# Transposes beside the output accumulators: a dynamic convolution and a two-matmul block on one Trainium2 core

## The chip, the cores and the metric

The kernel runs on one core of a Trainium2 chip (trn2). Times are device microseconds of one execution. The engines are named as in the profile: PE is TensorE's matmul, PEld its weight load, DVE is VectorE, ACT is ScalarE, POOL is GpSimd, SP issues most of the DMAs.

## The reference, cut to what matters

```python
# x (8, 4096, 192), weight_gen (8, 4096, 8 heads, 7), w_in (192, 2048), w_out (2048, 192)
w = softmax(weight_gen)                       # over the 7 taps, for each token and head
x_pad = concat(zeros(6 tokens), x)            # causal window of 7 tokens
conv[b, s, h, g] = sum_k w[b, s, h, k] * x_pad[b, s + k, h, g]     # 24 channels in a head
h = conv.reshape(32768, 192) @ w_in
out = (h - tanh(h)) @ w_out
```

## The kernel before

**Tiling.** The 32,768 tokens are cut into 32 superblocks of 1,024 tokens; a partition holds 8 consecutive tokens (J = 8). The work of a superblock is a convolution, whose result is transposed so that channels lie on partitions (`convT`), a first matmul (`gemm1`, 16 tiles f of 128 hidden columns), tanh and subtraction, and a second matmul (`gemm2`, 8 blocks of 128 tokens).

**Convolution.** ScalarE takes the exponential of the weights (`softmax_exp`, L117). VectorE sums over the taps and takes the reciprocal (`softmax_norm`, L127 and L131). GpSimd multiplies the exponentials by the reciprocal (`wsm`, L138), and then makes seven products of x and the weights of one tap, 128x1536 each (L156), into three tiles: `even` (taps 0, 2, 4), `odd` (1, 3, 5) and `last` (6). A DMA from GpSimd's queue then adds most of `odd` onto `even` (L165). TensorE transposes and sums what is left in PSUM by matmuls with the identity (`conv`, L194): 104 matmuls of 64x64 a superblock, in two groups, for channel chunks (0, 1) and (2,). The matmuls work in pairs: row tile r = 0 takes partitions 0 to 63, r = 1 takes 64 to 127, each with a PSUM bank of its own. ScalarE copies each group to `convT` (L204). For superblock 0 five of the seven products are VectorE's (taps 1, 3, 4, 5, 6).

**Matmuls.** `gemm1(n, f)` fills a tile `ph` of two banks (L217); ScalarE takes its tanh (`th`, L226) and VectorE subtracts (`gt`, L228). `gemm2(i)` multiplies block i by the upper half of w_out's contraction rows (r = 0), in a new bank `po`, and finishes block i-1 (r = 1) in the bank of the call before (L248); ScalarE then copies the finished block to `out_sb` (L273). A `po` tile is a whole bank of 512 columns, of which 192 are used.

**PSUM.** [...] `psum_h` has three slots of two banks, for `ph` and for the transposes' `pc` alike; `psum_o` has two slots of one bank for `po`. The tiles of most SBUF pools have two buffers.

**Order.** The order of each engine's instructions is written out by hand. In superblock n the loop over p = 0 to 7 issues two gemm1 tiles and, for the superblock before, one gemm2. GpSimd makes the products of superblock n+2, SP loads superblock n+3. The exponential of n+3 stands at p = 1, its sum and reciprocal at p = 2. The transposes of superblock n+1 stand at p = 2 and 5, up to n = 3 both at p = 7:

```python
if n + 1 < NTOT:
    if p == (2 if n > 3 else 7):
        conv(n + 1, (0, 1))
    if p == (5 if n > 3 else 7):
        conv(n + 1, (2,))
```

An engine works through its instructions in order: where one waits, all behind it wait.

Of the kernel before, what the change touches and what calls it, by code (L numbers as in the profile page):

```python
# [8 lines left out]
FP32 = mybir.dt.float32  # L9
BF16 = mybir.dt.bfloat16  # L10

ACT = mybir.ActivationFunctionType
# [4 lines left out]
def kernel(  # L17
# [8 lines left out]
    nc = tc.nc  # L26
# [15 lines left out]
    NFT = F // P  # L42
    NC = D // R
    GC = G // NC
    NPAIR = K // 2
    ACC = NPAIR * J * D - J * R
    assert S % TOK == 0 and D % R == 0 and H * GC == R and F % P == 0
# [19 lines left out]
    wg_of = {}  # L67
    e_of = {}
    zr_of = {}
    prods_of = {}  # L70
    conv_of = {}
    g_of = {}
# [48 lines left out]
        )  # L121
        e_of[n] = e_t

    def softmax_norm(n):
        e_t = e_of.pop(n)
        zsum = wgpool.tile([P, J * H], FP32, name="zsum")
        nc.vector.reduce_sum(  # L127
            out=zsum[:], in_=e_t[:].rearrange("p j h k -> p (j h) k"), axis=AX.X
        )
        zr = wgpool.tile([P, J * H], FP32, name="zr")  # L130
        nc.vector.reciprocal(zr[:], zsum[:])  # L131
        zr_of[n] = (e_t, zr)

    def products(n, on_vector=(), hooks={}):
        x_t = x_of.pop(n)
        e_t, zr = zr_of.pop(n)
        wsm = wgpool.tile([P, J, H, K], FP32, name="wsm")
        nc.gpsimd.tensor_mul(  # L138
            wsm[:].rearrange("p j h k -> p (j h) k"),
            e_t[:].rearrange("p j h k -> p (j h) k"),  # L140
            zr[:].rearrange("p (n o) -> p n o", o=1).to_broadcast([P, J * H, K]),
        )

        even = ppool.tile([P, NPAIR, NC, J, H, GC], BF16, name="even")
        odd = ppool.tile([P, NPAIR, NC, J, H, GC], BF16, name="odd")
        last = ppool.tile([P, NC, J, H, GC], BF16, name="last")
        dst = {}
        for i in range(NPAIR):
            dst[2 * i] = even[:, i]
            dst[2 * i + 1] = odd[:, i]  # L150
        dst[K - 1] = last[:]
        if -1 in hooks:
            hooks[-1]()
        for k in range(K):
            eng = nc.vector if k in on_vector else nc.gpsimd
            eng.tensor_mul(  # L156
                dst[k].rearrange("p c j h g -> p j h c g"),
                x_t[:, k : k + J, :].rearrange("p j (h c g) -> p j h c g", h=H, c=NC),
                wsm[:, :, :, k : k + 1]
                .rearrange("p j h (k o) -> p j h k o", o=1)  # L160
                .to_broadcast([P, J, H, NC, GC]),
            )
            if k == K - 2:

                nc.gpsimd.dma_start(  # L165
                    out=even[:].rearrange("p i c j h g -> p (i c j h g)")[:, 0:ACC],
                    in_=odd[:].rearrange("p i c j h g -> p (i c j h g)")[:, 0:ACC],
                    accum_op=mybir.AluOpType.add,
                    max_dma_last_dim=4096,
                )  # L170
            if k in hooks:
                hooks[k]()
        groups = [even[:, i] for i in range(NPAIR)] + [last[:]]
        prods_of[n] = [groups + ([odd[:, NPAIR - 1]] if c == NC - 1 else []) for c in range(NC)]

    def conv(n, chunks):

        prods = prods_of[n]
        if n not in conv_of:
            conv_of[n] = cpool.tile([P, NC, HT], BF16, name="convT")  # L180
        convT = conv_of[n]
        nch = len(chunks)
        pc = psum_h.tile([P, 2, HT], FP32, name="pc", tag="ph")
        steps = [
            (gi, ci, c)
            for gi in range(NPAIR + 2)
            for ci, c in enumerate(chunks)
            if gi < len(prods[c])
        ]
        for si, (gi, ci, c) in enumerate(steps):  # L190
            for j in range(JH):
                col = (ci * JH + j) * R
                for r in range(2):
                    nc.tensor.matmul(  # L194
                        pc[:, r, col : col + R],
                        lhsT=prods[c][gi][r * R : (r + 1) * R, c, 2 * j : 2 * j + 2].rearrange(
                            "p j h g -> p (j h g)"
                        ),
                        rhs=ident[r * R : (r + 1) * R, r * R : (r + 1) * R],
                        start=(si == 0 and j == 0),  # L200
                        stop=(si == len(steps) - 1 and j == JH - 1),
                    )
        c0 = chunks[0]
        nc.scalar.activation(  # L204
            out=convT[:, c0 : c0 + nch, :].rearrange("p c (j r t) -> p r (c j) t", r=2, t=R),
            in_=pc[:, :, 0 : nch * JH * R].rearrange("p r (cj t) -> p r cj t", t=R),
            func=ACT.Copy,
        )
        if c0 + nch == NC:
            prods_of.pop(n)  # L210

    def gemm1(n, f):
        convT = conv_of[n]
        ph = psum_h.tile([P, 2, HT], FP32, name="ph", tag="ph")
        for c in range(NC):
            for r in range(2):
                nc.tensor.matmul(  # L217
                    ph[:, r, :],
                    lhsT=w_in[r * R : (r + 1) * R, c, f * P : (f + 1) * P],
                    rhs=convT[r * R : (r + 1) * R, c, :],  # L220
                    start=(c == 0),
                    stop=(c == NC - 1),
                )
        th = tpool.tile([P, TOK], FP32, name="th")
        ph_f = ph[:].rearrange("p r t -> p (r t)")
        last_act[0] = nc.scalar.activation(out=th[:], in_=ph_f, func=ACT.Tanh)  # L226
        gt = gpool.tile([P, TOK], BF16, name=f"gt{f}", tag=f"gt{f}")
        nc.vector.tensor_sub(gt[:], ph_f, th[:])  # L228
        g_of.setdefault(n, []).append(gt)
# [5 lines left out]
    def gemm2(i):  # L235

        ops = []
        for r, blk in ((0, i), (1, i - 1)):
            if not 0 <= blk < LAST:
                continue  # L240
            n, j = divmod(blk, J)
            if r == 0:
                half[blk] = psum_o.tile([P, 512], FP32, name="po")
            ops.append((r, n, j, half[blk]))
        for f in range(NFT):
            for r, n, j, po in ops:
                col = (j % 2) * HT + (j // 2) * P
                mm = nc.tensor.matmul(  # L248
                    po[:, 0:D],
                    lhsT=g_of[n][f][r * R : (r + 1) * R, col : col + P],  # L250
                    rhs=w_out[r * R : (r + 1) * R, f, :],
                    start=(r == 0 and f == 0),
                    stop=(r == 1 and f == NFT - 1),
                )
                if r == 1 and f == 0 and i in (1, LAST):


                    tc.add_manual_dep(
                        mm.ins,
                        last_act[0].ins.name,  # L260
                        mybir.DependencyInfo(
                            mybir.DependencyClass.Sync, mybir.DependencyReason.DATA
                        ),
                        reason="order of the row tiles in a bank",
                    )
        if i > 0:
            blk = i - 1
            n, j = divmod(blk, J)
            po = half.pop(blk)
            if j == 0:  # L270
                out_of[n] = opool.tile([P, J, D], FP32, name="out_sb")
            out_sb = out_of[n]
            last_act[0] = nc.scalar.activation(out=out_sb[:, j, :], in_=po[:, 0:D], func=ACT.Copy)  # L273
            if j == J - 1:
                out_of.pop(n)
                g_of.pop(n)
                nc.sync.dma_start(
                    out=out[n * TOK : (n + 1) * TOK, :].rearrange("(p j) e -> p j e", p=P),
                    in_=out_sb[:],
                )  # L280
# [62 lines left out]
    for n in range(NTOT):  # L343
        if n + 3 < NTOT:
            load(n + 3)
        if n + 2 < NTOT:
            products(n + 2)
        for p in range(J):
            gemm1(n, 2 * p)
            gemm1(n, 2 * p + 1)  # L350
            if p == 1 and n + 3 < NTOT:
                softmax_exp(n + 3)
            if n >= 1:
                gemm2((n - 1) * J + p)
            if n + 1 < NTOT:
                if p == (2 if n > 3 else 7):
                    conv(n + 1, (0, 1))
                if p == (5 if n > 3 else 7):
                    conv(n + 1, (2,))
            if p == 2 and n + 3 < NTOT:  # L360
                softmax_norm(n + 3)
    gemm2(LAST)
    for j in range(J):
        gemm2_last(j)
# [30 lines left out]
```

The softmax here doesn't subtract the row's maximum and nothing guards it: scores larger than these inputs give would overflow.

## Time and profile before

| | |
|---|---|
| median of 3 runs | 806.3 us (803.76 to 807.86) |
| profiled execution | 803.36 us, of which the span is 801.5 us |
| TensorE clock granted | 0.997 of full speed |
| busy in the span: PE, DVE, ACT, POOL | 738.3, 653.4, 644.2, 707.2 us |
| transposes (L194), matmuls | 3,328 |
| copies to convT (L204) | 32 of 1,024 ns, 32 of 597 ns |
| wsm on POOL (L138) | 32 of 1,392 ns |
| adding DMA even<-odd | 32, 8.9 us from issue to landing |

A busy share is an average over the whole span. The timeline of a stretch gives the start and the duration of each instruction, merged where several of a kind follow each other ("x12"), and in brackets how long the engine was idle before it and what ended the idle time. The chain that ended last is followed back from the last instruction: at each step to what released it.

### The profile page before, as it was taken

The numbers are of one execution on the slowest core, as the hardware profiler recorded it, in microseconds if no ns is written. First come the engines' busy times: TensorE is split into PE (matmuls) and PEld (weight loads), VectorE is DVE, ScalarE is ACT, GpSimd is POOL, SyncE is SP. The second block draws the span as 40 slices with busy tenths as digits, with TensorE's granted clock in tenths as the row PEclk, the third lists the DMA queues.
The fourth block names the chain that finished last, engine by engine and source line by source line (L and its number), as shares of the span: only waits on it lengthen the run. The fifth ranks groups of instructions, "written<-read, shape, count | busy, mean of one in ns | idle before, by whom it ended". The sixth has DMA issues, their size and how long they took to land.

```text
span 801.5 us, 31993 instructions
## 1 busy us (share of the span) xinstructions
PE 738.3 (92%) x14592; PEld 570.1 (71%) x14592; DVE 653.4 (82%) x590; ACT 644.2 (80%) x865; POOL 707.2 (88%) x298
## 2 busy tenths in 40 slices
PE   0269999799999999999999999999999999999997
PEld 0227777577777777777777777777777777777777
DVE  5397877688888888888888888888888888887883
ACT  0187888688888888888888888888888888888883
POOL 7799999999999999999999999999999999996000
PEclk9999999999999999999999999999999999999999
DMA  8785555566665555576656654675654556634112
GB/s 165 220 172 119 106 136 152 150 171 174 175 170 112 141 147 149 155 175 174 170 128 147 141 149 146 168 174 143 156 147 125 150 155 175 163 55 95 42 41 81
DMA packets 25990, 114.50 MB, mean 143 GB/s; under 512 B 4688, under 2 KB 9344, under 8 KB 21704
## 3 DMA queue, kind: packets, MB, share of 16 engines
q1 hardware_dynamic: 14576, 77.34, 28.1%
q0 software_dynamic: 11280, 35.13, 27.1%
q8 instruction: 114, 1.87, 1.0%
q14 instruction: 20, 0.16, 0.1%
HBM read 54.49 MB, written 25.17 MB: 99 GB/s over the span
## 4 chain that ended last, share of the span: by engine, by line
PE 74%; DVE 13%; ACT 5%; DMA 4%; POOL 3%; issue 1%; SPq 0%; DVEq 0%; POOLq 0%; ACTq 0%
PE ph L217 35%; PE po L248 34%; DVE gt L228 11%; ACT th L226 4%; PE pc L194 4%; DMA even<-odd 3%; PE po L289 1%; POOL even L156 1%; POOL odd L156 1%; DMA x_t<-in_x_dram 1%; DVE odd L156 1%; POOL last L156 0%; ACT convT L204 0%; DVE even L156 0%; DVE zr L131 0%
## 5 line engine op out<-in xcount | busy, mean ns | idle before, releaser
L228 DVE TENSOR_TENSOR gt<-ph,th 128x1024 bf16<-128x1024 f32 x512 | 602.2, 1219 | 110.7 <-ACT th L226 107.8
L226 ACT ACTIVATE th<-ph 128x1024 f32<-128x1024 f32 x512 | 500.6, 1023 | 62.1 <-PE ph L217 57.1
L217 PE MATMUL ph<-convT,w_in 64*128 64x512 bf16 x3072 | 391.0, 377 | 17.8 <-DVE gt L228 16.1
L248 PEld LDWEIGHTS <-gt 64*128 64x128 bf16 x7936 | 344.3, 94 | 54.1 <-ACT th L226 1.7
L248 PE MATMUL po<-w_out,gt 64*128 64x192 bf16 x7936 | 374.6, 243 | 2.5 <-ACT th L226 1.3
L156 POOL TENSOR_TENSOR even<-x_t,wsm 128x1536 bf16<-128x1536 f32 x95 | 277.9, 2925 | 7.6 <-POOL wsm L138 6.1
L156 POOL TENSOR_TENSOR odd<-x_t,wsm 128x1536 bf16<-128x1536 f32 x93 | 269.9, 2902 | 0.0
L217 PEld LDWEIGHTS <-w_in 64*128 64x128 bf16 x3072 | 169.6, 94 | 133.3 <-issue 43.4
L156 POOL TENSOR_TENSOR last<-x_t,wsm 128x1536 bf16<-128x1536 f32 x31 | 104.3, 3364 | 0.0
L273 ACT ACTIVATE out_sb<-po 128x192 f32<-128x192 f32 x248 | 82.1, 331 | 19.1 <-PE po L248 13.1
L204 ACT ACTIVATE convT<-pc 128x1024 bf16<-128x1024 f32 x64 | 51.4, 810 | 45.8 <-PE pc L194 45.7
L194 PE MATMUL pc<-ident,even 64*128 64x64 bf16 x2304 | 46.6, 192 | 39.2 <-DMA even<-odd 38.9
L194 PEld LDWEIGHTS <-even 64*128 64x128 bf16 x2304 | 43.6, 97 | 39.9 <-issue 39.6
L165 POOL DMA_DIRECT2D even<-odd x32 | 38.6, 1205 | 13.5 <-POOL odd L156 9.6
L138 POOL TENSOR_TENSOR wsm<-e_t,zr 128x448 f32<-128x448 f32 x32 | 44.5, 1392 | 5.1 <-DVE zr L131 5.1
L117 ACT ACTIVATE e_t<-wg_t 128x448 f32<-128x448 f32 x32 | 18.5, 578 | 18.4 <-DMA wg_t<-in_weight_gen_dram 18.4
L127 DVE TENSOR_REDUCE zsum<-e_t 128x64 f32<-128x448 f32 x32 | 19.5, 609 | 16.6 <-ACT e_t L117 16.6
L194 PE MATMUL pc<-ident,last 64*128 64x64 bf16 x768 | 23.6, 193 | 0.0
L131 DVE RECIPROCAL zr<-zsum 128x64 f32<-128x64 f32 x32 | 17.7, 553 | 3.1
L194 PEld LDWEIGHTS <-last 64*128 64x128 bf16 x768 | 17.3, 97 | 0.1
L156 DVE TENSOR_TENSOR odd<-x_t,wsm 128x1536 bf16<-128x1536 f32 x3 | 7.9, 2654 | 5.0 <-DMA x_t<-in_x_dram 5.0
L289 PE MATMUL po<-w_out,gt 64*128 64x192 bf16 x256 | 11.0, 243 | 0.0
(17 smaller groups left out, 47.2 us busy)
## 6 DMA issues: line engine op xcount, KB each, us to landing
even<-odd POOLq DMA_DIRECT2D x32, 1024.0 KB, 8.9
x_t<-in_x_dram SPq DMA_DIRECT2D x24, 1344.0 KB
out_dram<-out_sb SPq DMA_DIRECT2D x31, 768.0 KB
x_t<-in_x_dram SPq DMA_DIRECT2D x8, 1176.0 KB
wg_t<-in_weight_gen_dram SPq DMA_DIRECT2D x32, 224.0 KB
x_t<-in_x_dram SPq DMA_DIRECT2D x8, 157.5 KB
w_in<-in_moe_w_in_dram POOLq DMA_DIRECT2D x8, 96.0 KB, 5.7
w_in<-w_in SPq DMA_DIRECT2D x2, 384.0 KB
```

The source lines that it names most:

```text
L127: nc.vector.reduce_sum(out=zsum[:], in_=e_t[:].rearrange("p j h k -> p (j h) k"), axis=AX.X)
L138: nc.gpsimd.tensor_mul(wsm[:].rearrange("p j h k -> p (j h) k"), e_t[:].rearrange("p j h k -> p (j h) k"), zr[:].rearrange("p (n o) -> p n ...
L156: eng.tensor_mul(dst[k].rearrange("p c j h g -> p j h c g"), x_t[:, k : k + J, :].rearrange("p j (h c g) -> p j h c g", h=H, c=NC), wsm[:, ...
L165: nc.gpsimd.dma_start(out=even[:].rearrange("p i c j h g -> p (i c j h g)")[:, 0:ACC], in_=odd[:].rearrange("p i c j h g -> p (i c j h g)" ...
L194: nc.tensor.matmul(pc[:, r, col : col + R], lhsT=prods[c][gi][r * R : (r + 1) * R, c, 2 * j : 2 * j + 2].rearrange("p j h g -> p (j h g)") ...
L204: nc.scalar.activation(out=convT[:, c0 : c0 + nch, :].rearrange("p c (j r t) -> p r (c j) t", r=2, t=R), in_=pc[:, :, 0 : nch * JH * R].re ...
L217: nc.tensor.matmul(ph[:, r, :], lhsT=w_in[r * R : (r + 1) * R, c, f * P : (f + 1) * P], rhs=convT[r * R : (r + 1) * R, c, :], start=(c == ...
L226: last_act[0] = nc.scalar.activation(out=th[:], in_=ph_f, func=ACT.Tanh)
L228: nc.vector.tensor_sub(gt[:], ph_f, th[:])
L248: mm = nc.tensor.matmul(po[:, 0:D], lhsT=g_of[n][f][r * R : (r + 1) * R, col : col + P], rhs=w_out[r * R : (r + 1) * R, f, :], start=(r == ...
L273: last_act[0] = nc.scalar.activation(out=out_sb[:, j, :], in_=po[:, 0:D], func=ACT.Copy)
L289: nc.tensor.matmul(po[:, r, 0:D], lhsT=g_of[n][f][r * R : (r + 1) * R, col : col + P], rhs=w_out[r * R : (r + 1) * R, f, :], start=(f == 0 ...
```

## The change

- The transposes of superblock n+1 (n >= 1) no longer take a slot of `psum_h`. They are cut into three groups, one for a channel chunk, at p = 2, 4 and 6 from n = 1 on (`conv_beside`), and write columns 192 to 447 of the two `po` banks that gemm2 has just used: r = 0 in that of block i, r = 1 in that of block i-1. Each group has two copies to `convT`, one for a bank. Superblocks 0 and 1 still use `conv`.
- The exponential of superblock n+3 moves to p = 4, its sum and reciprocal to p = 6. From superblock 4 on the reciprocal is written to columns 448 to 511 of block i's `po` bank, and VectorE, not GpSimd, multiplies it with the exponentials.
- For superblock 0 VectorE makes its own scaled weights, in a slot of `psum_h`, and GpSimd makes those of its two products.
- For superblocks 0, 1 and 2 (`PLAIN`) the adding DMA is left out. TensorE sums all seven products, 168 matmuls in place of 104, in the order in which the products come.

```diff
+    PLAIN = (0, 1, 2)
...
-    def softmax_norm(n):
+    def softmax_norm(n, po=None):
...
+        zr = po[:, 512 - J * H : 512]
+        nc.vector.reciprocal(zr, zsum[:])
+        wsm = wgpool.tile([P, J, H, K], FP32, name="wsm")
+        scale(nc.vector, wsm[:], e_t, zr)
+        wsm_of[n] = wsm
...
+            if on_vector:
+                pw = psum_h.tile([P, 2, HT], FP32, name="pw", tag="ph")
+                wsm_v = pw[:, 0, 0 : J * H * K].rearrange("p (j h k) -> p j h k", j=J, h=H)
+                scale(nc.vector, wsm_v, e_t, zr[:])
+            wsm = wgpool.tile([P, J, H, K], FP32, name="wsm")
+            scale(nc.gpsimd, wsm[:], e_t, zr[:])
+        in_pairs = n not in PLAIN
...
-            eng = nc.vector if k in on_vector else nc.gpsimd
+            eng, w = (nc.vector, wsm_v) if k in on_vector else (nc.gpsimd, wsm[:])
...
-            if k == K - 2:
+            if k == K - 2 and in_pairs:
                 nc.gpsimd.dma_start(
...
+            prods_of[n] = [[dst[k] for k in sorted(range(K), key=lambda k: (k in on_vector, k))]] * NC
...
+    def conv_beside(n, c, pos):
+        convT = conv_tile(n)
+        banks = [po[:, D : D + JH * R] for po in pos]
+        transposes(n, (c,), banks, False)
+        for r in range(2):
+            nc.scalar.activation(
+                out=convT[:, c, :].rearrange("p (j r t) -> p r j t", r=2, t=R)[:, r],
+                in_=banks[r].rearrange("p (j t) -> p j t", t=R),
+                func=ACT.Copy,
+            )
...
-            if p == 1 and n + 3 < NTOT:
+            if p == 4 and n + 3 < NTOT:
                 softmax_exp(n + 3)
             if n >= 1:
-                gemm2((n - 1) * J + p)
-            if n + 1 < NTOT:
-                if p == (2 if n > 3 else 7):
-                    conv(n + 1, (0, 1))
-                if p == (5 if n > 3 else 7):
-                    conv(n + 1, (2,))
-            if p == 2 and n + 3 < NTOT:
-                softmax_norm(n + 3)
+                gemm2(i)
+            if n == 0 and p == J - 1:
+                conv(1, (0, 1))
+                conv(1, (2,))
+            elif n >= 1 and n + 1 < NTOT and p in (2, 4, 6):
+                conv_beside(n + 1, p // 2 - 1, (half[i], half[i - 1]))
+            if p == 6 and n + 3 < NTOT:
+                softmax_norm(n + 3, half[i] if n >= 1 else None)
```

`scale` is the multiplication that `products` held before, on the engine that it is given. `transposes` holds the matmul loop of `conv` before, and writes to the banks that it is given; beside gemm2's columns its first matmul does not carry the start flag[...].

More of the change, by code (lines that the diff above doesn't have):

```diff
@@ L69 @@
     zr_of = {}
+    wsm_of = {}
     prods_of = {}
@@ L129, in softmax_norm, with scale @@
         )
-        zr = wgpool.tile([P, J * H], FP32, name="zr")
-        nc.vector.reciprocal(zr[:], zsum[:])
-        zr_of[n] = (e_t, zr)
+        if po is None:
+            zr = wgpool.tile([P, J * H], FP32, name="zr")
+            nc.vector.reciprocal(zr[:], zsum[:])
+            zr_of[n] = (e_t, zr)
+            return
+        zr = po[:, 512 - J * H : 512]
[3 more added lines that the diff above has]
+        wsm_of[n] = wsm
+    def scale(eng, wsm, e_t, zr):
+        eng.tensor_mul(
+            wsm.rearrange("p j h k -> p (j h) k"),
+            e_t[:].rearrange("p j h k -> p (j h) k"),
+            zr.rearrange("p (n o) -> p n o", o=1).to_broadcast([P, J * H, K]),
+        )
     def products(n, on_vector=(), hooks={}):
         x_t = x_of.pop(n)
[L136 to L142, printed above, removed]
+        wsm_v = None
+        if n in wsm_of:
+            wsm = wsm_of.pop(n)
+        else:
+            e_t, zr = zr_of.pop(n)
+            if on_vector:
[5 more added lines that the diff above has]
+        in_pairs = n not in PLAIN
         even = ppool.tile([P, NPAIR, NC, J, H, GC], BF16, name="even")
@@ L158, in products @@
                 x_t[:, k : k + J, :].rearrange("p j (h c g) -> p j h c g", h=H, c=NC),
-                wsm[:, :, :, k : k + 1]
+                w[:, :, :, k : k + 1]
                 .rearrange("p j h (k o) -> p j h k o", o=1)
@@ L172, in products @@
                 hooks[k]()
[L173 to L178, printed above, removed]
+        if in_pairs:
+            groups = [even[:, i] for i in range(NPAIR)] + [last[:]]
+            prods_of[n] = [
+                groups + ([odd[:, NPAIR - 1]] if c == NC - 1 else []) for c in range(NC)
+            ]
+        else:
+            prods_of[n] = [[dst[k] for k in sorted(range(K), key=lambda k: (k in on_vector, k))]] * NC
@@ L179, in conv, with conv_tile, transposes @@
+    def conv_tile(n):
         if n not in conv_of:
             conv_of[n] = cpool.tile([P, NC, HT], BF16, name="convT")
-        convT = conv_of[n]
+        return conv_of[n]
+    def transposes(n, chunks, banks, start):
+        prods = prods_of[n]
+        steps = [
+            (gi, ci, c, j)
+            for gi in range(max(len(prods[c]) for c in chunks))
+            for ci, c in enumerate(chunks)
+            if gi < len(prods[c])
+            for j in range(JH)
+        ]
+        for si, (gi, ci, c, j) in enumerate(steps):
+            col = (ci * JH + j) * R
+            for r in range(2):
+                nc.tensor.matmul(
+                    banks[r][:, col : col + R],
+                    lhsT=prods[c][gi][r * R : (r + 1) * R, c, 2 * j : 2 * j + 2].rearrange(
+                        "p j h g -> p (j h g)"
+                    ),
+                    rhs=ident[r * R : (r + 1) * R, r * R : (r + 1) * R],
+                    start=(start and si == 0),
+                    stop=(si == len(steps) - 1),
+                    skip_group_check=not start,
+                )
+        if chunks[-1] == NC - 1:
+            prods_of.pop(n)
@@ L182, in conv @@
+    def conv(n, chunks):
+        convT = conv_tile(n)
         nch = len(chunks)
         pc = psum_h.tile([P, 2, HT], FP32, name="pc", tag="ph")
[L184 to L202, printed above, removed]
+        transposes(n, chunks, (pc[:, 0], pc[:, 1]), True)
@@ L208, in conv @@
         )
-        if c0 + nch == NC:
-            prods_of.pop(n)
+    def conv_beside(n, c, pos):
+        convT = conv_tile(n)
+        banks = [po[:, D : D + JH * R] for po in pos]
+        transposes(n, (c,), banks, False)
+        for r in range(2):
+            nc.scalar.activation(
+                out=convT[:, c, :].rearrange("p (j r t) -> p r j t", r=2, t=R)[:, r],
+                in_=banks[r].rearrange("p (j t) -> p j t", t=R),
+                func=ACT.Copy,
+            )
     def gemm1(n, f):
@@ L265, in gemm2 @@
                     )
+        half.pop(i - 2, None)
         if i > 0:
@@ L268, in gemm2 @@
             n, j = divmod(blk, J)
-            po = half.pop(blk)
+            po = half[blk]
             if j == 0:
@@ L348 @@
         for p in range(J):
+            i = (n - 1) * J + p
             gemm1(n, 2 * p)
             gemm1(n, 2 * p + 1)
-            if p == 1 and n + 3 < NTOT:
+            if p == 4 and n + 3 < NTOT:
                 softmax_exp(n + 3)
             if n >= 1:
-                gemm2((n - 1) * J + p)
-            if n + 1 < NTOT:
-                if p == (2 if n > 3 else 7):
-                    conv(n + 1, (0, 1))
-                if p == (5 if n > 3 else 7):
-                    conv(n + 1, (2,))
-            if p == 2 and n + 3 < NTOT:
-                softmax_norm(n + 3)
+                gemm2(i)
[6 more added lines that the diff above has]
+                softmax_norm(n + 3, half[i] if n >= 1 else None)
     gemm2(LAST)
```

## Prediction

> **What bounds the kernel now.** I read the page first (shares, then the chain that ended last), then TensorE's timeline of one steady superblock with ScalarE's and VectorE's beside it, then GpSimd's start.
>
> From the page:
>
> ```profile
> PE 738.3 (92%) x14592; PEld 570.1 (71%) x14592; DVE 653.4 (82%) x590; ACT 644.2 (80%) x865; POOL 707.2 (88%) x298
> ...
> PE 74%; DVE 13%; ACT 5%; DMA 4%; POOL 3%; issue 1%; SPq 0%; DVEq 0%; POOLq 0%; ACTq 0%
> ...
> L204 ACT ACTIVATE convT<-pc 128x1024 bf16<-128x1024 f32 x32 | 32.8, 1024 | 38.9 <-PE pc L194 38.9
> ```
>
> TensorE carries 74% of the chain. Now its timeline around the second transpose group of a superblock (start, duration, engine, line):
>
> ```profile
> 338.71 1.48 PE L217 MATMUL ph<-convT,w_in 64*128 64x512 bf16 x12
> 340.00 1.50 PE L248 MATMUL po<-w_out,gt 64*128 64x192 bf16 x32
> 341.32 0.53 PE L194 MATMUL pc<-ident,even 64*128 64x64 bf16 x24
> 341.67 0.30 PE L194 MATMUL pc<-ident,last 64*128 64x64 bf16 x8
> 341.79 0.30 PE L194 MATMUL pc<-ident,odd 64*128 64x64 bf16 x8
> 341.91 0.83 PE L217 MATMUL ph<-convT,w_in 64*128 64x512 bf16 x6
> 343.04 0.82 PE L217 MATMUL ph<-convT,w_in 64*128 64x512 bf16 x6 [0.30 <-DVE gt L228]
> ```
>
> Starts tell more than durations, since ends are modelled. A pair of gemm1 tiles issues in 1.29 us, a gemm2 in 1.32, so one p takes 2.61; the 40 transposes take 0.59 (14.6 ns each), the 64 of the other group 0.93. TensorE runs without a hole up to 341.91. Eight p and 104 transposes make 8 x 2.61 + 1.52 = **22.4 us**; the measured period is 23.12 (VectorE's pair after the second group starts at 340.63, 363.75, 386.86). The missing 0.7 us is the price of lending an h slot to each of the two transpose groups: 0.30 in the last line, the rest in slower gemm1 pairs after each group. What runs beside:
>
> ```profile
> 339.57 1.94 ACT L226 ACTIVATE th<-ph 128x1024 f32<-128x1024 f32 x2 [0.32 <-PE ph L217]
> 341.54 0.33 ACT L273 ACTIVATE out_sb<-po 128x192 f32<-128x192 f32 x1
> ...
> 352.92 0.58 ACT L117 ACTIVATE e_t<-wg_t 128x448 f32<-128x448 f32 x1
> 353.39 0.33 ACT L273 ACTIVATE out_sb<-po 128x192 f32<-128x192 f32 x1
> ```
>
> ```profile
> 340.63 2.36 DVE L228 TENSOR_TENSOR gt<-ph,th 128x1024 bf16<-128x1024 f32 x2 [0.33 <-ACT th L226]
> ```
>
> With the p's first gemm1 at 338.71 as zero, gemm2 is issued by +2.61, the copy of its finished block to out_sb ends at +3.16, the gt pair ends at +4.28. The transposes at 341.32 did not wait for that copy: they had a tile of their own.
>
> In the chain before 150 us the limit is GpSimd and its adding DMA:
>
> ```profile
> 132.48 2.87 POOL odd L156
> 135.35 0.29 issue
> 135.65 9.34 DMA even<-odd
> 144.99 0.14 issue
> 145.12 1.89 PE pc L194 x64
> 147.01 1.93 PE ph L217 x12
> ```
>
> GpSimd's period is 22.64 us (wsm at 48.73, 71.38, 94.01), less than TensorE's, so from there on TensorE alone sets the pace.
>
> **What the skill says.** "PSUM — Partial Sum Buffer", section "PSUM bank collisions raise a hardware error": engines are to be guarded by bank, not by address. No row of before shows two engines wanting disjoint columns of one bank. It decides here: the changed kernel's instructions as built carry such waits. "SBUF — State Buffer", "Who interferes with whom": a VectorE operation with two SBUF inputs contends with GpSimd's reads, one with a single SBUF input does not. The trace agrees: of the VectorE products (both inputs in SBUF) those beside a GpSimd product took 4.45 us, those alone 1.74. "TensorE: Matmul & The Clock Gate", "Why this matters for your kernels": an idle gap of over about 3 us lowers the clock. Agrees: after the 4.14 us gap that ends at 145.12 the granted clock was 0.52 for 3.2 us.
>
> **The change, part by part.**
>
> *Prologue (gain).* The weights that VectorE's five products read go to PSUM, so these no longer collide: 10.17 + 5 x 1.68 (spacing of the last two) = 18.6 instead of 24.0. GpSimd's two products end at 17. The adding DMA (22.95 to 34.6) is gone; 64 more transposes cost under 2 us, mostly beside the products. So gemm1 starts near 20.5 instead of 37.74 (w_in must have come; the bandwidth slices suggest about 20). But tanh 0 stands behind exp 2 on ScalarE, whose weights I expect near 25: they are queued behind superblock 1's x. Then the first gt comes near 26.7, not 40.26. Gain there 13.6.
>
> *Superblocks 0 to 3 (gain given back).* GpSimd's products(1) start at about 24.1 (before 26.33; gated by exp 1 at 20.97, zsum, reciprocal, wsm), take 7 x 2.86 + 1.21 for w_out and end at 45.3. TensorE reaches conv(1) at 57.41 - 13.6 = 43.8, waits to 45.3, and superblock 1 starts at about 46.7 (before 59.68). But conv(2) now stands at p = 2 of superblock 1, in TensorE's order, no longer at p = 7. TensorE arrives near 58.6 (before it took 59.68 to 71.63 to get there); products(2) end at 45.3 + 1.5 (wsm) + 20.0 = 66.7. An 8 us stall, plus some 1.6 for the low clock after it (64 transposes took 1.89 at 145.12, 0.93 otherwise; the next 12 matmuls 1.93, not 1.3). With 13.1 for five p, 1.6 for the other transposes and 2.6 of the waits below, superblock 2 starts near 85.8 (before 85.09): all of the gain is lost. There conv(3) needs the DMA add: 66.7 + 1.5 + 17.2 + 0.3 = 85.6 issued, + 9.3 = 94.9 landed; TensorE arrives at 85.8 + 3 x 2.61 = 93.6. Then 1.5 of transposes, 13.1 and 2.6: superblock 3 starts near **112.1 (before 109.0): 3 us worse.** The three DMA issues that are left out free GpSimd's queue by only 0.8 us each (45.07 to 45.86), and SP's queue keeps its order. Afterwards GpSimd without wsm needs 22.64 - 1.5 = 21.1 a superblock. The later softmax (p = 6) lets products(n+3) start 24.3 us into superblock n; their DMA lands 26.7 later, 8 us ahead of conv(n+3) two superblocks on. So GpSimd is off the path, and the 4.1 us wait at 145 goes too.
>
> *Steady superblock.* Removed: transposes from the h slots, so 0.7 us of holes. Added waits, read off the changed kernel's order:
>
> 1. In each of the three groups the first transpose to the older bank waits for ScalarE's out_sb copy of that bank, which gemm2 has just finished. Copy ends at +3.16, signal about 0.05 (as between gt's end at 342.99 and TensorE's 343.04), transposes would have started at +2.61: **0.60 us** at p = 2 and 6. At p = 4 the exp stands before it on ScalarE: in the lines above (gemm2 issued 350.23 + 2.61 = 352.84, copy ends 353.72) that is 0.88 + 0.05 = **0.93**. Behind it on TensorE stands everything: gemm1 of the next p, hence tanh and gt.
> 2. At p = 6 VectorE's reciprocal writes the younger bank and its scaling reads it; the next gemm2 starts in it and waits for the scaling. gt pair to +4.28; zsum, reciprocal as in before (0.61, 0.55 with gaps: +5.45); scaling 448 elements, by the gt row's 1219 ns for 1024 at one per cycle of "VectorE: DVE Perf Modes" (0.96 GHz): estimate 0.62, ends +6.17. TensorE would be there at 2.61 + 0.60 + 0.59 + 1.31 = +5.1: **1.05 us**. VectorE's next gt comes 0.45 late, which nobody misses.
> 3. Six ScalarE copies of 128x256 (estimate 0.38, from 331 ns at 192 and 597 at 512) replace 1.02 + 0.60: +0.7 us. They end 0.9 us after the transposes; the next gemm2, which needs them, comes after 1.31. Cost nothing while that 0.4 us lasts; if not, up to 0.3 per group. ScalarE (20.0 busy in a steady superblock) + 0.7 and VectorE (19.9) + 0.6 stay below the period.
>
> Period: 22.4 + 0.60 + 0.93 + 0.60 + 1.05 = **25.6**, i.e. 2.4 more than before's mean of 23.18 (154.61 to 757.21, the same VectorE pair 26 superblocks on). The lower bound of the waits (no signal time, reciprocal and scaling faster by 0.3) is 2.6 instead of 3.2; the upper (restart 0.1 each, slower PSUM write, convT copies late) 3.9.
>
> *Sum.* Superblocks 3 to 28: 26 x 25.6 = 665; 29 and 30 have no softmax, 24.2 each. Superblock 31 starts at 112.1 + 665 + 48 = 825; before at 764.2. The tail is the same. 61 us more on the span of 801.5, so 862.6, and 864.4 with the 1.86 around it. The profiled execution (803.36) lies 2.9 under the median of the runs, so **867**.
>
> **Rivals.**
>
> - *The waits are already over when TensorE arrives* (the transposes interleave cleanly). Then only the holes go: superblock 3 near 112.1 - 2.6 = 109.5, 28 x 22.4 more gives 737 at superblock 31 instead of 764: 27 us faster, 779. For it: a wait in the order costs only what its signal is late, and ScalarE and VectorE have 3 us of slack a superblock. Against: ScalarE's copy cannot start before gemm2's end, and the rows show 0.55 between gemm2's last issue and the copy's end. It decides from the point at which the four waits together are under the 0.7 us of holes.
> - *Gains and waits cancel* (0.7 us of waits in all): within 0.5%. Would need most waits absent; little speaks for it.
> - *Worse than the sum*: ScalarE lags and its convT copies hold gemm2 too, or recurring gaps lower the clock. 0.5 us in three places x 28 is 42 more: 909. Against: TensorE was idle a quarter of superblock 0 in before at clock 1.00.
> - *The start decides alone* (change without effect in the steady part): about 803; counted with "cancel".
>
> **Numbers.** The forecast 0.80, worse 0.10, the first rival 0.07, cancelled 0.03. The range 843 to 890 is the bounds of the waits (26 x -0.6 to 26 x +0.7) and about 5 us for the start; it leaves out most of the rivals. Slower by over 0.5% (about what a measurement of this kernel can tell from no change) 0.90, within 0.03, faster 0.07.
>
> **What would show it.** gemm1's first start near 20.5; a TensorE wait on the DMA-free products near 58 to 67; 90 TensorE waits on out_sb of 0.6 us (0.9 in a third of them); 28 waits on wsm of about 1 us; a period near 25.6; no wait on gt left. Wrong if the period is under 23.2, if the waits on out_sb are absent, or if GpSimd comes back onto the chain after 150 us.

## The result, and the profile after

The changed kernel takes 868.57 us (median, 868.36 to 869.06), the kernel before 805.86 us beside it: 1.078 times the time (95% interval 1.075 to 1.081), so **7.8% slower**. The profiled execution of the changed kernel has a span of 866.8 us, 65.3 us more than before.

From the page of the changed kernel, busy shares, the chain that ended last, and the group of the transposes with the idle time before them:

```profile
PE 754.2 (87%) x14784; PEld 575.7 (66%) x14784; DVE 664.7 (77%) x619; ACT 655.9 (76%) x985; POOL 675.7 (78%) x267
...
PE 62%; DVE 15%; ACT 10%; POOL 5%; issue 4%; DMA 3%; SPq 0%; DVEq 0%; ACTq 0%; POOLq 0%
...
L221 PE MATMUL po<-ident,even 64*128 64x64 bf16 x2160 | 63.2, 190 | 48.7 <-ACT out_sb L321 45.0
```

No engine has become the bound: every share has fallen. TensorE has new holes (stretches in which it stands idle), and the chain now passes from it to ScalarE (10%, before 5%) and back. Who it waits for stands in the waits of the changed kernel (us in total, times, longest):

```profile
PE po L221 <- ACT out_sb L321: 45.0, 89, 0.7
...
PE po L295 <- DVE wsm L145: 26.0, 28, 1.3
...
PE ph L264 <- DVE gt L275: 8.1, 11, 4.8
```

There are ninety groups of transposes and 89 waits on the out_sb copy; there are 28 scalings and 28 waits. The wait on gt came 44 times before, about once a superblock; the eleven that are left all lie in superblock 0. TensorE's timeline over the same part of a steady superblock (p = 2, then p = 4, then p = 6 and 7):

```profile
404.44 0.19 PE L221 MATMUL po<-ident,even 64*128 64x64 bf16 x1
405.05 0.51 PE L221 MATMUL po<-ident,even 64*128 64x64 bf16 x23 [0.42 <-ACT out_sb L321]
...
410.73 0.19 PE L221 MATMUL po<-ident,even 64*128 64x64 bf16 x1
411.64 0.51 PE L221 MATMUL po<-ident,even 64*128 64x64 bf16 x23 [0.72 <-ACT out_sb L321]
...
417.33 0.19 PE L221 MATMUL po<-ident,even 64*128 64x64 bf16 x1
417.92 0.51 PE L221 MATMUL po<-ident,even 64*128 64x64 bf16 x23 [0.40 <-ACT out_sb L321]
...
419.78 0.24 PE L295 MATMUL po<-w_out,gt 64*128 64x192 bf16 x1
420.95 1.48 PE L295 MATMUL po<-w_out,gt 64*128 64x192 bf16 x31 [0.92 <-DVE wsm L145]
```

The first matmul goes to the younger bank (that of block i), and the second, which goes to the older one (block i-1), stands. Taken from start to start, the waits are 0.61, 0.91, 0.59 and 1.17 us; the figure in brackets counts from the modelled end of the matmul before. ScalarE and VectorE at p = 6:

```profile
417.53 0.33 ACT L321 ACTIVATE out_sb<-po 128x192 f32<-128x192 f32 x1
418.68 0.66 ACT L253 ACTIVATE convT<-po 128x256 bf16<-128x256 f32 x2 [0.82 <-PE po L221]
```

```profile
416.62 2.36 DVE L275 TENSOR_TENSOR gt<-ph,th 128x1024 bf16<-128x1024 f32 x2 [0.26 <-ACT th L273]
418.89 0.61 DVE L129 TENSOR_REDUCE zsum<-e_t 128x64 f32<-128x448 f32 x1
419.61 0.56 DVE L139 RECIPROCAL po<-zsum 128x64 f32<-128x64 f32 x1
420.27 0.62 DVE L145 TENSOR_TENSOR wsm<-e_t,po 128x448 f32<-128x448 f32 x1
```

The copy ends at 417.86 and TensorE goes on at 417.92; the scaling ends at 420.89 and TensorE goes on at 420.95. The time from one reciprocal to the next, called the period below, is 25.64 us nearly throughout (23.12 before).

### The profile page after: what moved, and what is told of

The parts are those of the page before. It is cut to its first block, busy times and chain, and to the rows that moved or that the text cites. A ratio compares the mean times of both kernels' runs of the same rounds, so it can differ in the third digit from the quotient of the medians.

```text
span 866.8 us, 32494 instructions
## 1 busy us (share of the span) xinstructions
PE 754.2 (87%) x14784; PEld 575.7 (66%) x14784; DVE 664.7 (77%) x619; ACT 655.9 (76%) x985; POOL 675.7 (78%) x267
## 4 chain that ended last, share of the span: by engine, by line
PE 62%; DVE 15%; ACT 10%; POOL 5%; issue 4%; DMA 3%; SPq 0%; DVEq 0%; ACTq 0%; POOLq 0%
PE po L295 29%; PE ph L264 28%; DVE gt L275 9%; ACT th L273 7%; PE po L221 4%; ACT out_sb L321 2%; POOL even L178 2%; DVE wsm L145 2%; POOL odd L178 2%; DVE zsum L129 2%; DVE po L139 2%; ACT e_t L119 2%; PE po L337 1%; DMA even<-odd 1%; DMA wg_t<-in_weight_gen_dram 1%
## 5 line engine op out<-in xcount | busy, mean ns | idle before, releaser
L295 PE MATMUL po<-w_out,gt 64*128 64x192 bf16 x7936 | 381.2, 243 | 27.7 <-DVE wsm L145 26.0
L264 PE MATMUL ph<-convT,w_in 64*128 64x512 bf16 x3072 | 382.4, 378 | 8.9 <-DVE gt L275 8.1
L253 ACT ACTIVATE convT<-po 128x256 bf16<-128x256 f32 x180 | 59.2, 381 | 77.1 <-PE po L221 77.1
L221 PE MATMUL po<-ident,even 64*128 64x64 bf16 x2160 | 63.2, 190 | 48.7 <-ACT out_sb L321 45.0
L221 PEld LDWEIGHTS <-even 64*128 64x128 bf16 x2304 | 48.5, 95 | 81.0 <-issue 61.3
L119 ACT ACTIVATE e_t<-wg_t 128x448 f32<-128x448 f32 x32 | 18.5, 577 | 21.9 <-DMA wg_t<-in_weight_gen_dram 21.9
L221 PE MATMUL po<-ident,last 64*128 64x64 bf16 x720 | 26.0, 191 | 2.5 <-POOL last L178 2.5
L145 DVE TENSOR_TENSOR wsm<-e_t,po 128x448 f32<-128x448 f32 x28 | 17.4, 622 | 2.9
L221 PE MATMUL pc<-ident,even 64*128 64x64 bf16 x144 | 4.8, 214 | 17.0 <-POOL even L178 16.7
L139 DVE RECIPROCAL po<-zsum 128x64 f32<-128x64 f32 x28 | 15.7, 561 | 3.2 <-DVE zsum L129 0.5
L221 PE MATMUL po<-ident,odd 64*128 64x64 bf16 x304 | 10.8, 191 | 3.0 <-POOL odd L178 3.0
```

The costliest lines, as they stand in the source:

```text
L119: nc.scalar.activation(out=e_t[:].rearrange("p j h k -> p (j h k)"), in_=wg_t[:].rearrange("p j h k -> p (j h k)"), func=ACT.Exp,)
L145: eng.tensor_mul(wsm.rearrange("p j h k -> p (j h) k"), e_t[:].rearrange("p j h k -> p (j h) k"), zr.rearrange("p (n o) -> p n o", o=1).to ...
L221: nc.tensor.matmul(banks[r][:, col : col + R], lhsT=prods[c][gi][r * R : (r + 1) * R, c, 2 * j : 2 * j + 2].rearrange("p j h g -> p (j h g)"),
L253: nc.scalar.activation(out=convT[:, c, :].rearrange("p (j r t) -> p r j t", r=2, t=R)[:, r], in_=banks[r].rearrange("p (j t) -> p j t", t= ...
L264: nc.tensor.matmul(ph[:, r, :], lhsT=w_in[r * R : (r + 1) * R, c, f * P : (f + 1) * P], rhs=convT[r * R : (r + 1) * R, c, :], start=(c == ...
L295: mm = nc.tensor.matmul(po[:, 0:D], lhsT=g_of[n][f][r * R : (r + 1) * R, col : col + P], rhs=w_out[r * R : (r + 1) * R, f, :], start=(r == ...
```

## The experiments

All times are medians; ratios are to the kernel before on the same chip. The first six start from the changed kernel, the last four from its start alone.

**GpSimd scales again.** This takes away the wait of gemm2 on VectorE, and the scaling itself from VectorE.

```diff
-                softmax_norm(n + 3, half[i] if n >= 1 else None)
+                softmax_norm(n + 3)
```

> Edit: from superblock 4 on, the sum and reciprocal go to SBUF tiles again and GpSimd scales; everything else as in the changed kernel. Theory (the PSUM waits are the loss): the 28 TensorE waits on VectorE's scaling, 1.17 us each by starts (419.78 to 420.95), go, 27 of them outside the start: about 31 us less, so 837 us, and a period of 25.6 - 1.15 = 24.45. GpSimd's period is back at 22.6, still below that. Rival (GpSimd needs the relief): GpSimd comes back onto the chain after 150 us, and the time falls by less than 15 us or rises. Rival (VectorE's later gt is what holds TensorE, not the bank): the time falls by a few us only.

Measured: 837.84 us, ratio 1.041 (1.039 to 1.043), 30.7 less than the changed kernel; period 24.48. The waits on the scaling are gone, those on out_sb stay (44.6 us, 89 times). The time is as the theory had it, and GpSimd did not need the relief. But the edit does two things at once; the sixth experiment parts them, and puts 22.6 of the 31 us down to the bank.

**The exponential one p earlier.** This changes one wait without touching a bank.

```diff
-            if p == 4 and n + 3 < NTOT:
+            if p == 3 and n + 3 < NTOT:
                 softmax_exp(n + 3)
```

> Edit: the exponential of superblock n+3 stands at p = 3 in place of 4; nothing else. Theory (TensorE waits for the out_sb copy, and the exponential stands before that copy on ScalarE): the wait at p = 4 falls from 0.91 to 0.60 us, 30 x 0.31 = 9 us less (28 of them have an exponential, so 8.7): 860 us. Rival (the wait at p = 4 is longer for another cause, such as the transposes' data): 868 unchanged.

Measured: 860.49 us, ratio 1.069 (1.067 to 1.071), 8.1 less; period 25.32, 0.32 less. In its waits the longest on out_sb fell from 0.7 to 0.4:

```profile
PE po L221 <- ACT out_sb L321: 36.0, 89, 0.4
```

What is written to the banks is the same. So the length of the wait depends on where the copy stands in ScalarE's order.

**The copy made twice.** This doubles the suspected cost at the 90 groups.

```diff
             elif n >= 1 and n + 1 < NTOT and p in (2, 4, 6):
+                nc.scalar.activation(
+                    out=out_of[n - 1][:, p - 1, :], in_=half[i - 1][:, 0:D], func=ACT.Copy
+                )
                 conv_beside(n + 1, p // 2 - 1, (half[i], half[i - 1]))
```

> Edit: the out_sb copy of block i-1 is made twice in a row ahead of each of the 90 groups of transposes beside the output. Theory: TensorE waits for the end of the second copy, 0.25 to 0.33 us later each time, while ScalarE has about 5 us of slack a superblock: 90 x 0.29 = 26 us more, about 894 us; waits on out_sb in the trace of 0.9 us (1.2 at p = 4). Rival (the wait in the trace is really gemm2's drain or the switch of banks, and ScalarE's copy only ends at the same time): about 868, up to 872.

Measured: 890.50 us, ratio 1.106 (1.104 to 1.108), 21.9 more. From its waits and from the timeline of one group:

```profile
PE po L221 <- ACT out_sb L408: 78.2, 90, 1.1
```

```profile
413.51 0.19 PE L221 MATMUL po<-ident,even 64*128 64x64 bf16 x1
414.52 0.51 PE L221 MATMUL po<-ident,even 64*128 64x64 bf16 x23 [0.78 <-ACT out_sb L408]
```

The group waits 1.01 us, not 0.61, and now for the second copy (L408). So the copy's end is what releases TensorE. The period rose by 0.73, not by 3 x 0.40: at p = 6 the later transposes use up 0.4 us in which TensorE would have waited for the scaling.

**Transposes in h slots again, scaling as changed.**

```diff
-            if n == 0 and p == J - 1:
-                conv(1, (0, 1))
-                conv(1, (2,))
-            elif n >= 1 and n + 1 < NTOT and p in (2, 4, 6):
-                conv_beside(n + 1, p // 2 - 1, (half[i], half[i - 1]))
+            if n + 1 < NTOT:
+                if p == (2 if n >= 1 else 7):
+                    conv(n + 1, (0, 1))
+                if p == (5 if n >= 1 else 7):
+                    conv(n + 1, (2,))
```

> Edit: from superblock 1 on the transposes take a slot of the h pool again, in two groups at p = 2 and 5 as in the kernel before; 1/sum stays in the output bank, scaling on VectorE at p = 6. Theory: the three waits on out_sb (0.60 + 0.91 + 0.60 = 2.1 us a superblock) go and the holes of the h slots (0.7) come back: 1.4 us x 28 = 39 less, about 829 us, no TensorE wait on out_sb but a few, the 28 waits on the scaling stay. Rival (what costs is the transposes' place and number of groups, or writing beside live columns, not the wait): no row shows it, and the time stays near 868 or falls by under 15.

Measured: 849.13 us, ratio 1.055 (1.053 to 1.058): 19.4 less, half of what was expected. The waits on out_sb are gone, but in its timeline the other has grown:

```profile
411.22 0.24 PE L295 MATMUL po<-w_out,gt 64*128 64x192 bf16 x1
413.07 1.48 PE L295 MATMUL po<-w_out,gt 64*128 64x192 bf16 x31 [1.61 <-DVE wsm L145]
```

From start to start this is 1.85 in place of 1.17. With no group at p = 6, TensorE comes to gemm2 earlier, and VectorE is no sooner. 1.4 - 0.7 = 0.7 us a superblock are left (period 24.95 against 25.64). The expectation added two waits that overlap; the mechanism stands.

**Both undone.** The two edits above together.

> Edit: transposes in slots of the h pool at p = 2 and 5 from superblock 1 on, and GpSimd scales with 1/sum in SBUF; the new start, the exponential at p = 4 and the sum at p = 6 stay. Theory (the PSUM waits are the whole loss of the steady part): the period is that of the kernel before, 23.2 us; superblock 3 starts at about 114 as in the changed kernel, so superblock 31 at 114 + 28 x 23.2 = 764, where the kernel before had 764.2: 804 us, the same as before within 0.5%. Rival (the move of the softmax to p = 4 and 6, or the start, has a cost of its own): a period above 23.6 or over 812 us. Against the run with GpSimd's scaling alone (837.8) this is 34 us less, which is what the transposes' waits cost where no wait on the scaling is near.

Measured: 817.70 us, ratio 1.015 (1.013 to 1.017): 51 of the 64 us are back, 13 are not. Many periods are 23.34, 0.22 over before's 23.12, which makes 6 us; in such a superblock the gemm1 pair after the sum at p = 6 takes 1.52 us (349.90 to 351.42), not 1.29. The rest is in superblocks of 24 to 25 in which TensorE stands between two matmuls, eleven times for over 0.4 us, 9.5 us together, like this in its timeline:

```profile
596.89 0.39 PE L221 MATMUL pc<-ident,last 64*128 64x64 bf16 x14
598.22 0.20 PE L221 MATMUL pc<-ident,last 64*128 64x64 bf16 x2 [0.94 <-issue]
```

"issue" means that the profile shows nothing it waited for. The kernel before has one such stop over 0.4 us after 100 us, the changed kernel none. So the two parts that carry the PSUM waits account for 51 us; the theory that they are the whole loss is off by these stops and by the place of the sum.

**1/sum in SBUF, scaling on VectorE.**

```diff
-        zr = po[:, 512 - J * H : 512]
-        nc.vector.reciprocal(zr, zsum[:])
+        zs = wgpool.tile([P, J * H], FP32, name="zr")
+        zr = zs[:]
+        nc.vector.reciprocal(zr, zsum[:])
```

> Edit: VectorE scales as in the changed kernel, but 1/sum lies in an SBUF tile, so gemm2 no longer waits for VectorE and both inputs of the scaling are in SBUF. Theory (such an operation stands behind GpSimd's product, as 4.45 against 1.74 us showed in the start of the kernel before): the scaling takes up to 2.7 us more, the next gt comes that much later and TensorE waits for the h slot some 1 to 2.3 us instead of 1.15 for the bank: 865 to 900 us, 885 the likeliest, and a scaling of 2 to 3.4 us in the trace. Rival (contention is small for 448 elements): the scaling stays near 0.62 us, the wait goes, and the time is that of GpSimd's scaling, about 838 us.

Measured: 846.01 us, ratio 1.051 (1.049 to 1.052): 22.6 less than the changed kernel; 885 was expected. The instructions of the tile wsm (count, minimum, median and maximum in ns):

```profile
L146 DVE TENSOR_TENSOR wsm<-e_t,zr x28: 625/625/1546, 85.8 to 756.8; 128x448 f32<-128x448 f32 x28
```

Nearly every scaling took 0.625 us: no contention. In the steady part GpSimd stands idle just then; its next products wait for this scaling, and start 0.14 us after its end (410.76, 410.90). The expectation took for granted that GpSimd is busy all the time.

This is the cleanest measure of the bank's wait: VectorE does the same work, only the place of 1/sum differs, and 22.6 us are back. The period is 24.76, and 24.48 where GpSimd scales. The 0.28 between them, 8 us in all, are the scaling on VectorE: the four subtractions behind it run without a break (410.68 to 415.32), and the gemm1 pair beside them takes 1.56 us (411.04 to 412.60), not 1.29. So the prediction's "which nobody misses" of VectorE's later gt holds only while TensorE stands at the bank anyway.

**The start alone**, with before's transposes, softmax and scaling (exponential at p = 1, sum at p = 2, both groups at p = 7 up to n = 3):

> Edit: only the start of the change (superblock 0's weights for VectorE in PSUM, no adding DMA for superblocks 0 to 2); transposes, softmax and scaling as in the kernel before, with its p = 7 up to n = 3. Theory (the early gain is given back to GpSimd): superblock 1 starts near 48.8 in place of 59.7, but at p = 2 of superblock 4 TensorE stands and waits for superblock 5's adding DMA, which lands near 96.9 + 2 x 22.65 + 0.5 = 142, 3 us earlier than the 145 of before: 802 us, 0.4% faster than before, with a TensorE wait of about 10 us there. Rival (the start's gain is carried to the end): 11 us faster, 795.

Measured: 802.05 us, ratio 0.996 (0.995 to 0.997). From its timeline:

```profile
142.28 1.31 PE L221 MATMUL pc<-ident,even 64*128 64x64 bf16 x48 [4.75 <-DMA even<-odd]
```

The DMA of superblock 5 lands at 142 as expected, and TensorE waits for it. The wait is half as long as expected, because TensorE had lost time earlier, 2.81 us of it in one stop at 102.43 that is put down to issue. So the start itself is worth 3 us; of the 10 us of lead at superblock 1 (49.52, before 59.68) the rest goes to GpSimd's pace.

**Late groups**: the start alone, groups at p = 5 and 6, PLAIN up to superblock 6.

> Edit: the kernel with the start alone, with the two transpose groups in h slots at p = 5 and 6 for all superblocks from n = 1 on, and no adding DMA up to superblock 6 (four superblocks more). Theory (after the start only GpSimd's lateness stands between the early gain and the end): superblock 1 starts near 48.8, conv(2) at 48.8 + 15.7 = 64.5 waits 4 us for products that end near 68.3, and from there TensorE sets the pace: 48.8 + 4 + 30 x 23.2 + 4 x 0.9 for the added transposes = 752 at superblock 31 instead of 764: 793 us, 1.5% faster than before. Rival (two groups one p apart cost more h-slot holes, or GpSimd stays the limit): 800 to 812 us.

Measured: 829.20 us, ratio 1.032 (1.028 to 1.035): a miss. Its periods are 24.6 and then 23.9, with stops on issue of up to 2.6 us each; and there is a hole after the sum at p = 2, where no transposes stand:

```profile
406.95 0.82 PE L264 MATMUL ph<-convT,w_in 64*128 64x512 bf16 x6 [0.53 <-DVE gt L275]
```

**The sum beside the group**: the same with `softmax_norm` at p = 5 in place of 2.

> Edit: the kernel with late groups (p = 5 and 6, no adding DMA up to superblock 6), with the sum and reciprocal moved from p = 2 to p = 5, where the first group stands. Theory (VectorE's 1.2 us of sum and reciprocal at p = 2 opened an h-slot hole of its own, 0.53 us at 406.95, which the kernel before hides under the group at p = 2): the period falls from 23.9 to about 23.4, 829 - 30 x 0.5 = 814 us. Rival (the two groups one p apart, and TensorE stops that the profile puts down to nothing but issue, make the period): 823 us or more.

Measured: 799.71 us (796.0 to 803.9), ratio 0.993 (0.991 to 0.995). The usual period is 23.18, shorter than the 23.4 that was expected, and the time is 14 us under the expected 814. **This kernel is the fastest of all here, 0.7% faster than the kernel before.** Of the 29 us against the late groups some 20 are the period (0.72 in 28 superblocks); the stops on issue are also fewer in the profiled execution (the slowest of its ten), 10.4 us in place of 16.7, and no run tells why. VectorE's 1.2 us of softmax cost TensorE 0.7 us a superblock at p = 2, alone, and next to nothing at p = 5, where TensorE is in its transposes anyway. At p = 6 of "both undone", also without transposes, they cost 0.22; what makes that place cheaper was not tested.

**Relief for GpSimd**: the start alone, VectorE scaling for superblocks 4 to 7 with 1/sum in SBUF, both groups at p = 7 up to n = 5.

> Edit: the kernel with the start alone, with two things more: for superblocks 4 to 7 VectorE scales the weights (1/sum in SBUF, at p = 2), and both transpose groups stay at p = 7 up to n = 5 in place of 3. Theory (GpSimd is late by about 5 us at superblock 5, where TensorE waited 4.75 us at 142.28, and four scalings of 1.5 us are what it lacks): no wait on the adding DMA is left at n = 6, superblock 6 starts at 129.5 + 2 x 23.9 = 177.3 and superblock 31 at 177.3 + 25 x 23.15 = 756, 6 us earlier than with the start alone: 796 us. Rival (GpSimd is busy here, so that VectorE's scaling stands behind its products, 1 to 2.9 us each, and holds gt; or the two groups at p = 7 cost what is won): 801 to 806 us.

Measured: 827.19 us, ratio 1.028 (1.026 to 1.031): this is the rival, and far worse than its numbers. VectorE's timeline, and GpSimd's:

```profile
95.91 12.97 DVE L146 TENSOR_TENSOR wsm<-e_t,zr 128x448 f32<-128x448 f32 x1
108.81 3.47 DVE L276 TENSOR_TENSOR gt<-ph,th 128x1024 bf16<-128x1024 f32 x3
```

```profile
96.48 3.35 POOL L179 TENSOR_TENSOR even<-x_t,wsm 128x1536 bf16<-128x1536 f32 x1
99.34 3.34 POOL L179 TENSOR_TENSOR odd<-x_t,wsm 128x1536 bf16<-128x1536 f32 x1
102.20 3.33 POOL L179 TENSOR_TENSOR even<-x_t,wsm 128x1536 bf16<-128x1536 f32 x1
105.06 3.33 POOL L179 TENSOR_TENSOR odd<-x_t,wsm 128x1536 bf16<-128x1536 f32 x1
108.69 1.22 POOL L188 DMA_DIRECT2D even<-odd  x1 [0.30 <-POOL odd L179]
```

One scaling stood behind four products in a row, until GpSimd paused for its DMA, and TensorE behind it for 13.66 us. GpSimd lost nothing by it: its products start 2.86 us apart, as they do elsewhere. The other three scalings took 1.37, 3.37 and 3.37 us. Here, where GpSimd is late and works without a break, 1/sum in PSUM might have its use (not tested); in the steady part it has none.

## Why the prediction was right

The measured 868.6 us lies 1.6 from the forecast of 867. The mechanism and its terms were right, but so close a hit is in part luck. The sum gave a span of 862.6, and 866.8 was measured, 4.2 more. The forecast then added 2.9 because the profiled execution of before lay that far under its median; in the changed kernel the two agree (868.58 and 868.57), so the 2.9 happened to cover most of what was missing.

- **Waits on out_sb**: 0.60 at p = 2 and 6, 0.93 at p = 4; measured 0.61, 0.59, 0.91. The doubled copy and the moved exponential show that TensorE waits for the copy's end.
- **Wait on the scaling**: 1.05; measured 1.17 from start to start, of which one matmul slot (0.04) is TensorE's own. The scaling took 622 ns (estimate 0.62) and ended where the sum said, 6.18 us after the first gemm1 of the p (+6.17). With 1/sum in SBUF 22.6 us went; with the scaling on GpSimd too, 31.
- **Holes of the h slots**: said to go; waits on gt fell from 44 to 11, all of them in superblock 0.
- **Six convT copies**: 381 ns each (0.38), hidden as costed; no gemm2 waits for them in the list.
- **Period**: 25.6; measured 25.64. The rule of the Trainium skill, "PSUM — Partial Sum Buffer", section "PSUM bank collisions raise a hardware error", is to guard by bank and not by address; the program as built waits in that way, although the columns are disjoint. The runs show what these waits cost (3.24 us over the 22.4 of TensorE's own work). Whether the chip needs them at disjoint columns no run here shows, since none left them out.
- **Weights in PSUM**: said to free VectorE's products from GpSimd's. The one at 14.78 took 1.75 us beside a product of GpSimd; with both inputs in SBUF such a product took 4.45.
- **The start**: gemm1 first at 22.54 (20.5 said), superblock 1 at 48.81 (46.7), 2 at 87.92 (85.8), 3 at 114.20 (112.1). The 2 us of superblock 1 and those after it come in at one step: products(1) were to start at 24.1, gated by wsm, but GpSimd then waited for x and started at 25.95. The x transfer's landing was not worked out. The 2 us of the first gemm1 have another source (VectorE's first product began at 11.44, not 10.17, also after a wait for x, and from the end of its last product to gemm1 it is 2.7 us, not 1.9), and superblock 1, which waits for products(1), does not feel them. After that the steps ran as told, the stall at p = 2 of superblock 1 included: the last products came one by one until 68.35 (66.7 said).
- **Sum**: superblock 31 starts at 829.5 (825). Of the 4.5 us, 2.1 are the start's, 1.0 the period's last 0.04 us, 26 times over, 0.35 one superblock of 25.99, and 1 is rounding in the sum.
- **Range**: by the bounds that are named for it, the lower end is 846, not 843 (867 - 15.6 - 5); nothing hangs on it.

What the sum did not show is that its waits are not independent: 0.6 us of the out_sb wait at p = 6 lies over the wait on the scaling. Added forward it came out right, since each was taken behind the one before it. Taken away singly they don't add up, as the fourth experiment found: the period falls by 1.16 (GpSimd scales again) and by 0.69 (transposes in h slots), and with both edits from 25.64 to a usual 23.34, by 2.30. That the times do seem to add up (31 and 19 singly, 51 together) is due to the stops on issue in that last run.

## What to carry to other kernels

A PSUM bank that looks half empty is not free space in a program that guards its banks as a whole: who writes the spare columns waits for every reader of the rest. Here three such waits of 0.6 to 0.9 us, 2.1 us a superblock, cost three times the 0.7 us of holes that they removed. Before work is moved into the shadow of another engine, look at what stands ahead of it in that engine's order, and at what TensorE does at that moment: the same 1.2 us on VectorE were nearly free beside a transpose group and cost 0.2 or 0.7 us without one. Waits that follow each other must be taken off together to see what each is worth.

## What the runs showed of the hardware that was not expected

- A VectorE multiplication with both inputs in SBUF (448 elements) took 0.625 us while GpSimd was idle and up to 12.97 us while GpSimd ran product after product. In that case it did not take turns with them: the four products started 2.86 us apart, as without it. Their recorded 3.35 us in place of 2.90 is not its doing, for the products at 87.89, 90.76 and 93.62, before it began, have 3.35 to 3.38 too. Two others stood for 3.37 us, about one product; what decides between one product and four is not shown.
- TensorE stops on "issue" of 0.4 to 3.9 us appear again and again in some of the kernels that keep it busy (both undone, late groups, the sum beside the group), a few times in the start alone, once in the kernel before, and never in the changed kernel, where it waits for others in every superblock. In the run with both parts undone, a 16 KB packet of the instruction queue (q8) starts 2.2 to 2.8 us before the end of each of the eleven stops; there are 115 such packets in its 815 us. That TensorE had run out of instructions fits this, but no run tested it; why the kernel before has fewer stays open.
